# A banded attention in pieces of 128, 96 and 8 keys, four heads at a time, in front of two mixture-of-experts layers

## The chip, the cores and the metric

The kernel runs on one core of a Trainium2 chip. The time is that of one execution on the device, in microseconds; smaller is better. The core's engines are named as the profile names them: PE (TensorE, matrix products; PEld is its weight load), DVE (VectorE), ACT (ScalarE), POOL (GpSimd) and SP, which here only issues DMAs. Each engine takes its instructions in the order of the program and stops at one that has to wait.

## The reference

Attention over 2 batches, 8 heads, 768 positions and 64 numbers per head; its output, 1536 rows of 512, goes through a first mixture of 8 experts, whose weights come out of eight rounds of normalising (Sinkhorn), and a second one, in which each row goes to one expert.

```python
def _attn_ref(q, k, v, n_global, n_local):          # n_global 8, n_local 96
    scores = scale * np.matmul(q, k.transpose(0, 1, 3, 2))
    rel = pos[:, None] - pos[None, :]
    is_global = pos[None, :] < int(n_global)
    is_local = (rel >= 0) & (rel < int(n_local))
    keep = is_global | is_local
    dist = np.where(is_global & ~is_local, float(n_local), np.abs(rel))
    scores = np.where(keep, scores - slopes * dist, -1e9)
    a = softmax(scores)
    return np.matmul(a, v)
def _moe_ref(x, w_gate, w1, w2):
    P = sinkhorn(x @ w_gate)                          # 8 rounds over rows and columns
    for e in range(E):
        out += P[:, e:e + 1] * (np.maximum(x @ w1[e], 0.0) @ w2[e])
```

A query thus sees the 8 first keys and the 96 last ones up to its own. The second layer is the same two products on the rows that a greedy choice gives to each expert.

## The kernel before

The work has five stages: attention, Sinkhorn, the first layer (`hidden` and `expert_out`, by expert and by 512 rows), routing, and the second layer. Everything in the layers is done with float32 split into two half-precision parts, three products for one (`mm3`, L474 to L479).

Attention goes by 12 blocks of 128 queries (2 batches times 6). A block's keys are the 8 global ones, then 95 of the block before it, then its own 128: 231 columns (128 for the first block of a batch, whose table differs). They are kept in two pieces of 128 and 103. `load` (L213) fetches q, k and v of a block on SP's queue; v goes to `vb` in runs that end where a piece ends, so three DMAs of 8, 120 and 103 rows (L223). `qb` and `kb` have 2 buffers, `vb` has 3. `start` (L228) transposes q and k on PE; q is copied into two tiles of 128 rows whose other half is zero (`qtz`, L240), so that one head of a pair can be multiplied with all 128 rows of the pair's keys. `assemble` (L256) copies the keys into a `slab` on POOL.

A step handles two heads. `weigh` (L270): two score products on PE (L281), for each head an add of the bias table with a minimum (L284, DVE) and the exponential with its sum (L286, ACT), then the reciprocal (L288, L289, DVE) and the multiplication by it (L291, POOL). Two steps later `turn` (L293) transposes the weights on PE (L302) and copies them out of PSUM (L305 on DVE, L307 on ACT); two steps after that `mix` (L310) multiplies them with v (L319). Score banks in PSUM are two, by turns. When a block is whole, `split_x` (L322) takes a bound of its magnitudes on ACT (L499), turns it over PE (L103) into a power of two on DVE, and writes the two half-precision parts of x transposed (L333, L334) and the first gate's logits.

Between the steps stand parts of other stages: the first expert's two weight matrices (`early`, L416 loads, L420 the largest magnitude, L431 and L432 the two parts), in blocks 1 to 5 and 6 to 10, and from block 6 on two of the 16 pieces of the first expert's `hidden` per block, 14 in all. A program (the tile framework's scheduler) then sets the order on each engine; no order is written by hand.

After attention come the rest of `hidden` for expert 0, Sinkhorn (L519 to L539), and `expert_out(0, 0)`, whose DVE instruction (L572) needs Sinkhorn's result.

Of the kernel before, what the change touches and what calls it, by code (L numbers as in the profile page):

```python
# [10 lines left out]
F32 = mybir.dt.float32  # L11
# [29 lines left out]
def tile_sparse_attention_moe_moe(ctx, tc, q, k, v, ng, nl, wg1, w11, w12, wg2, w21, w22, out, taps=None):  # L41
# [19 lines left out]
    wide = WMAX > 240 or ng > P  # L61
# [53 lines left out]
    def split_gate(pool, g, kc, name):  # L115
        """[P, kc, (lo, hi, 0), E] fp16 parts of g and the scale."""
# [15 lines left out]
    def gate_product(hi, lo, hl, n, f, dst, plus=None):  # L132
        """dst[128, E] = f * sum over n chunks of (hi + lo)^T (g_hi + g_lo) [+ plus]."""
# [11 lines left out]
    def gate_block(hi, lo, sx, gw, dst):  # L145
        """dst[128 tokens, E] = x @ w_gate; hi, lo: kc -> [128, 128 tokens]."""
# [5 lines left out]
    # ------------------------------------------------------------- attention  # L152
# [6 lines left out]
    def attention(atp, aps):  # L159
        qtz = []  # L160
# [7 lines left out]
        def table(i):  # L168
            """-(bias) of the kept scores, 1e9 elsewhere, for the columns of block i."""
# [43 lines left out]
        def load(b, i):  # L213
            qb = rows(q, b, i, "qb")
            kb = rows(k, b, i, "kb") if not wide else None
            nch = (widths[i] + P - 1) // P
            vb = atp.tile([P, NCHM, H, D], F32, name="vb", bufs=3 if not wide else 2)
# [8 lines left out]
            return qb, kb, vb, nch  # L226

        def start(b, i):  # L228
            """Transposes of the block's queries and keys, and the keys that it sees."""
            c = b * NBLK + i  # L230
            qb, kb, vb, nch = lds.pop((b, i))
# [9 lines left out]
            if kb is not None:  # L241
                turn_keys(b, i, kb)
            return S

        def turn_keys(b, i, kb):
# [4 lines left out]
            if b == 0 and i < 4:  # L250
                nc.scalar.activation(kt, pt, AF.Copy)
            else:
                nc.vector.tensor_copy(kt, pt)
# [16 lines left out]
        def weigh(S, p):  # L270
            """The softmax of two heads' scores."""
            W = S.W
            ex = S.ex[p] = atp.tile([P, 2, WMAX], F32, name="ex", bufs=5 if not wide else 2)
# [20 lines left out]
        def turn(S, p):  # L294
            ex = S.ex.pop(p)
            ets = S.et[p] = []
            for a0 in range(0, S.nch, 2):
                pe = aps.tile([P, 2, 2, P], F32, name="pe", tag="tr", bufs=trb)
                for a in range(a0, min(S.nch, a0 + 2)):
# [3 lines left out]
                    et = atp.tile([P, 2, P], F32, name="et", bufs=4 if not wide else NCHM + 2)  # L303
# [6 lines left out]
        def mix(S, p):  # L310
            if p == 0:
                if S.c % 2 and not wide:
                    S.pa = mmbank([P, HP, P], name="pa")
                else:
                    S.pa = aps.tile([P, HP, P], F32, name="pa", tag="av", bufs=1)
# [6 lines left out]
        def split_x(c, pa):  # L322
            """The block's x^T in two parts and its logits, by steps."""
# [15 lines left out]

        order = [(b, i) for b in range(B) for i in range(NBLK)]  # L340
        lds = {}
        if wide:
            for b in range(B):
                for i in range(NBLK):
                    turn_keys(b, i, rows(k, b, i, "kb"))
                for i in range(NBLK):
                    lds[b, i] = load(b, i)
                    S = start(b, i)
                    assemble(S)
                    for p in range(HP):  # L350
                        weigh(S, p)
                        turn(S, p)
                        mix(S, p)
                    finish(split_x(S.c, S.pa))
            return
        warm = sml.tile([P, 1], F32, name="warm", bufs=1)
        nc.scalar.activation(warm, ones[:, 0:1], AF.Exp)
        lds[order[0]] = load(*order[0])
        table(0)
        table(min(1, NBLK - 1))  # L360
        blocks = {0: start(*order[0])}
        assemble(blocks[0])
        pairs = [(n, p) for n in range(len(order)) for p in range(HP)]
        splits = []
        with nullcontext():
            for t in range(len(pairs) + 4):
                n, p = divmod(t, HP)
                if n < len(order) and p == 0:
                    for m in (n + 1, n + 2):
                        if m < len(order) and m not in blocks and order[m] not in lds:  # L370
                            lds[order[m]] = load(*order[m])
                for z, (c0, c1, ps_) in enumerate(((1, 6, range(HP)), (6, 11, range(HP)))):
                    if c0 <= n < c1 and p in ps_:
                        next(early[z], None)
                    if (n, p) == (c1, 0):
                        finish(early[z])
                for x in splits:
                    next(x, None)
                if t < len(pairs):
                    weigh(blocks[n], p)  # L380
                if p == 0 and n + 1 < len(order):
                    blocks[n + 1] = start(*order[n + 1])
                    assemble(blocks[n + 1])
                if 0 <= t - 2 < len(pairs):
                    m, pp = pairs[t - 2]
                    turn(blocks[m], pp)
# [583 lines left out]
```

## Time and profile before

| | us |
|---|---|
| median of 3 runs | 1442.07 (1438.77 to 1445.28) |
| span of the profiled execution | 1442.0 (1442.01 with two digits) |
| first matrix product | 10.37 |
| last product of attention with v ends | 220.07 |
| first layer, routing and second layer | the rest |

The page gives no other time of the profiled execution than its span, which is 0.06 us from the median of the timed runs, so a sum made against the span is a sum against the median. Busy time is a union over an engine's instructions. In the windows, PEclk is the mean granted clock of PE, 1.00 being full, and DMA share is the mean busy share of the core's 16 DMA engines. In a wait row stand the total, the number of waits and the longest. A timeline row starts with its start and its duration, and ends with the idle time before it and what ended it. A float32 product that is no transpose has two records in the trace.

### The profile page before, as it was taken

The page shows a single profiled execution, that of the slowest core. Times are in us where ns is not written, and L with a number is a line of the kernel's source. Part 1 is how long each engine was busy: PE and PEld are TensorE (multiplying, and loading weights), DVE is VectorE, ACT ScalarE, POOL GpSimd, SP SyncE. Part 2 cuts the span into 40 slices and gives each one's busy share as a digit, 9 for nine tenths or more (in the row PEclk, how much of TensorE's full clock was granted, in tenths as well). Part 3 has the DMA queues.
Part 4 walks back from the last instruction along what each step waited for, and adds up shares of the span by engine and source line. Part 5 has one row for each costly group of instructions (what it writes and reads, how often), then busy time and mean ns, then how long its engine had stood idle before and what let it go on. Part 6 is the DMA issues. An engine that isn't in the chain of part 4 may idle for free.

```text
span 1442.0 us, 20217 instructions
## 1 busy us (share of the span) xinstructions
PE 1362.6 (94%) x7966; PEld 700.3 (49%) x7966; DVE 811.8 (56%) x1900; ACT 605.7 (42%) x1111; POOL 155.4 (11%) x289
## 2 busy tenths in 40 slices
PE   5777989999999999999999999999999999979998
PEld 4554654444444444444444444445555343337775
DVE  5555758656466656646665664575645786822111
ACT  4454745124324333432433353256553464613332
POOL 3232411101000100100010010000000000030000
PEclk9789989999999999999999999999999999999999
DMA  4444311334244415424441543341001111258640
GB/s 78 114 81 115 81 33 59 126 109 133 101 152 155 161 59 175 134 100 152 155 161 59 168 140 102 132 153 67 2 1 60 59 59 59 117 153 322 263 197 30
DMA packets 88332, 164.93 MB, mean 114 GB/s; under 512 B 49838, under 2 KB 49838, under 8 KB 85678
## 3 DMA queue, kind: packets, MB, share of 16 engines
q1 hardware_dynamic: 76814, 119.60, 26.5%
q0 software_dynamic: 11424, 44.05, 8.2%
q8 instruction: 62, 1.02, 0.3%
q14 instruction: 32, 0.26, 0.1%
HBM read 119.59 MB, written 44.05 MB: 113 GB/s over the span
## 4 chain that ended last, share of the span: by engine, by line
PE 55%; issue 13%; DMA 12%; DVE 10%; ACT 4%; SPq 3%; POOL 2%; POOLq 0%; ACTq 0%; DVEq 0%
PE py L477 9%; PE py L478 9%; PE py L479 9%; DMA raw<-in_moe_w_dram 8%; PE ph L477 6%; PE ph L479 6%; PE ph L478 6%; DMA ws<-spill 4%; DVE wam L420 2%; PE pr L761 2%; DVE wslot L432 2%; PE ps L281 2%; PE pa L319 1%; SPq L210 1%; DVE hslot L472 1%
## 5 line engine op out<-in xcount | busy, mean ns | idle before, releaser
L477 PE MATMUL py<-wslot,hslot 128*128 128x512 f16 x768 | 291.3, 379 | 9.5 <-ACT relu L471 9.0
L477 PE MATMUL ph<-xt,wslot 128*128 128x512 f16 x768 | 292.1, 380 | 0.8 <-DVE acc L574 0.7
L478 PE MATMUL ph<-xt,wslot 128*128 128x512 f16 x768 | 291.8, 380 | 0.0
L479 PE MATMUL ph<-xt,wslot 128*128 128x512 f16 x768 | 291.8, 380 | 0.0
L478 PE MATMUL py<-wslot,hslot 128*128 128x512 f16 x768 | 291.2, 379 | 0.0
L479 PE MATMUL py<-wslot,hslot 128*128 128x512 f16 x768 | 291.2, 379 | 0.0
L420 DVE TENSOR_REDUCE wam<-raw 128x1 f32<-128x1024 f32 (+1 forms) x136 | 153.1, 1151 | 93.1 <-DMA raw<-in_moe_w_dram 92.5
L470 ACT ACTIVATE hslot<-ph 128x512 f16<-128x512 f32 x192 | 114.4, 596 | 205.1 <-PE ph L479 204.9
L472 DVE TENSOR_TENSOR hslot<-relu,hslot 128x512 f16<-128x512 f32 x192 | 131.5, 688 | 112.8 <-ACT relu L471 111.9
L431 ACT ACTIVATE spill<-raw,s 128x1024 f16<-128x1024 f32 x64 | 72.9, 1147 | 235.8 <-DVE s L112 126.2
L432 DVE SCALAR_TENSOR_TENSOR spill<-raw,s,spill 128x1024 f16<-128x1024 f32 x64 | 81.6, 1283 | 108.5 <-ACT spill L431 107.3
L471 ACT ACTIVATE relu<-ph 128x512 f32<-128x512 f32 (+1 forms) x224 | 130.0, 580 | 0.0
L478 PEld LDWEIGHTS <-hslot 128*128 128x128 f16 x768 | 75.0, 98 | 100.8 <-issue 19.4
L477 PEld LDWEIGHTS <-hslot 128*128 128x128 f16 x768 | 75.0, 98 | 92.0 <-issue 10.3
L479 PEld LDWEIGHTS <-hslot 128*128 128x128 f16 x768 | 75.0, 98 | 89.9 <-issue 6.5
L479 PEld LDWEIGHTS <-wslot 128*128 128x128 f16 x768 | 75.2, 98 | 86.8 <-issue 0.8
L477 PEld LDWEIGHTS <-wslot 128*128 128x128 f16 x768 | 75.2, 98 | 86.6 <-issue 3.2
L478 PEld LDWEIGHTS <-wslot 128*128 128x128 f16 x768 | 75.2, 98 | 86.4 <-issue 2.6
L431 ACT ACTIVATE wslot<-raw,s 128x1024 f16<-128x1024 f32 (+1 forms) x72 | 71.5, 1047 | 73.1 <-PE py L479 72.6
L432 DVE SCALAR_TENSOR_TENSOR wslot<-raw,s,wslot 128x1024 f16<-128x1024 f32 (+1 forms) x72 | 81.7, 1163 | 5.0 <-ACT wslot L431 5.0
L574 DVE SCALAR_TENSOR_TENSOR acc<-py,pf,acc 128x512 f32<-128x512 f32 x84 | 61.4, 745 | 32.4 <-PE py L479 32.4
L463 POOL DMA_DIRECT2D ws<-spill x64 | 44.3, 694 | 214.8 <-DVE spill L432 214.5
(235 smaller groups left out, 1658.9 us busy)
## 6 DMA issues: line engine op xcount, KB each, us to landing
raw<-in_moe_w_dram SPq DMA_DIRECT2D x64, 1024.0 KB
ws<-spill POOLq DMA_DIRECT2D x64, 512.0 KB, 6.5
w2slot<-ws SPq DMA_DIRECT2D x16, 2048.0 KB
hd<-hslot POOLq DMA_DIRECT2D x2, 2048.0 KB, 7.8
hslot<-hd SPq DMA_DIRECT2D x2, 2048.0 KB
qb<-in_q_dram SPq DMA_DIRECT2D x12, 256.0 KB
kb<-in_k_dram SPq DMA_DIRECT2D x12, 256.0 KB
vb<-in_v_dram SPq DMA_DIRECT2D x12, 240.0 KB
```

The costliest lines, as they stand in the source:

```text
L281: nc.tensor.matmul(ps[:, j - j0, n0:n1], S.qz[:, j, p, :], S.slab[:, p, n0:n1], start=True, stop=True)
L420: nc.vector.tensor_reduce(am[:, y:y + 1], raw, axis=AX.X, op=ALU.max, apply_absolute_value=True)
L431: nc.scalar.activation(hi, raw, AF.Copy, scale=s[:, 0:1])
L432: nc.vector.scalar_tensor_tensor(lo, raw, s[:, 0:1], hi, op0=ALU.mult, op1=ALU.subtract)
L463: nc.gpsimd.dma_start(dr[:, :, a * q4:a * q4 + q4], t)
L470: nc.scalar.activation(hi, ps, AF.Relu, scale=HS)
L471: nc.scalar.activation(r[:, :n], ps, AF.Relu, scale=HS)
L472: nc.vector.tensor_sub(lo, r[:, :n], hi)
L477: nc.tensor.matmul(out_, lhs(0, a), rhs(0, a), start=a == 0, stop=False)
L478: nc.tensor.matmul(out_, lhs(0, a), rhs(1, a), start=False, stop=False)
L479: nc.tensor.matmul(out_, lhs(1, a), rhs(0, a), start=False, stop=a == n - 1)
L574: nc.vector.scalar_tensor_tensor(acc[:, c, :DM], ps, pf[:, c:c + 1], acc[:, c, :DM], op0=ALU.mult, op1=ALU.add)
```

## The change

The attention is rewritten for the case that a band and a few global keys are kept; the old function stays for other shapes and is not called. What is new:

- A block's keys stand in the order own 128, previous 96, global 8 (232 columns). v's own 128 rows (`vo`, 8 buffers) are loaded once per block, seven blocks ahead; the 96 and the 8 rows go to `vp` (3 buffers). `qb` and `kb` have 3 buffers. Keys reach the `slab` directly from PSUM by one DVE copy; POOL copies 96 and 8 columns from the slab before.
- q is not padded: one copy `qt`, and the two heads of a pair are multiplied in the upper and the lower 64 rows of the array (`tile_position`), each into its own PSUM bank.
- A step handles four heads: `turn` comes one step later, `mix` two. Each of the two score banks (`sc0`, `sc1`) has one buffer. Copies out of PSUM are 512 wide, not 256.
- The order in `mix` alternates the two halves of the output.
- The scale of x is one power of two per batch, from the largest magnitude of v (`magnitude`, a DVE reduction per block; `batch_scale`), instead of one per block from x itself.
- One more piece of `hidden`, 15, is placed between the steps. The table for 232 columns is made on POOL, clipped at 1e9.

```diff
-            vb = atp.tile([P, NCHM, H, D], F32, name="vb", bufs=3 if not wide else 2)
-                    nc.sync.dma_start(vb[p0:p0 + n, ch], v[b, :, s:s + n, :].rearrange("h p d -> p h d"))
+        def load_own(n):
+            if n < NB:
+                vos[n] = rows(v, n, "vo", 8)
+        def load(n):
+            qbs[n] = rows(q, n, "qb", 3)
+            kbs[n] = rows(k, n, "kb", 3)
+            b, i = order[n]
+            if i:
+                t = atp.tile([P, H, D], F32, name="vp", bufs=3)
+                nc.sync.dma_start(t[0:NP], v[b, :, i * P - NP:i * P, :].rearrange("h p d -> p h d"))
+                nc.sync.dma_start(t[NP:NP + ng], v[b, :, 0:ng, :].rearrange("h p d -> p h d"))
...
+            nc.vector.tensor_reduce(vams[b][:, i:i + 1], vos[n], axis=AX.XY, op=ALU.max, apply_absolute_value=True)
+        def batch_scale(b):
+            am = vams.pop(b)
+            nc.vector.tensor_reduce(am[:, NBLK:], am[:, :NBLK], axis=AX.X, op=ALU.max)
+            s = pow2_scale(am[:, NBLK:], "sv", bufs=2)
...
+            S.qt = atp.tile([P, HP, P], F32, name="qt", bufs=2)
+            nc.scalar.activation(S.qt, pt, AF.Copy, scale=qs)
+            nc.vector.tensor_copy(S.slab[:, :, 0:P], pt)
+                nc.gpsimd.tensor_copy(S.slab[:, :, P:P + NP], slabs.pop(n - 1)[:, :, P - NP:P])
+                nc.gpsimd.tensor_copy(S.slab[:, :, P + NP:], kgs[b])
...
-                ps = aps.tile([P, SJ, SW], F32, name="ps", tag="sc", bufs=2 if SW <= 256 else 1)
-                        nc.tensor.matmul(ps[:, j - j0, n0:n1], S.qz[:, j, p, :], S.slab[:, p, n0:n1],
+            ps = [aps.tile([P, 2, 256], F32, name=f"ps{j}", tag=f"sc{j}", bufs=1) for j in range(2)]
+            for y in range(HU):
+                for j in range(2):
+                    nc.tensor.matmul(ps[j][:, y, :W], S.qt[64 * j:64 * j + 64, HU * u + y, :],
+                                     S.slab[64 * j:64 * j + 64, HU * u + y, :W], start=True, stop=True,
+                                     tile_position=(64 * j, 0))
...
+                for a, ck in enumerate(S.cks):
+                    for j in range(2):
+                        nc.tensor.matmul(S.pa[64 * j:64 * j + 64, p, :], S.vs[a][:ck, 2 * p + j, :], ets[a][:ck, y, j, :],
+                                         start=a == 0, stop=a == S.nch - 1, tile_position=(0, 64 * j))
...
+            nc.scalar.activation(hi, S.pa, AF.Copy, scale=s[:, 0:1])
...
+        units = [(n, u) for n in range(NB) for u in range(2)]
+        for t in range(len(units) + 3):
+            if t < len(units):
+                weigh(blocks[n], u)
+            if u == 0 and n + 1 < NB:
+                blocks[n + 1] = start(n + 1)
+            if 0 <= t - 1 < len(units):
+                turn(blocks[m], x)
+            if 0 <= t - 2 < len(units):
+                mix(blocks[m], x)
+            if n >= 6 and first_hidden:
+                hidden(*first_hidden.pop(0))
```

The diff says little of the order on the engines, so two places are shown. The first is SP's queue near the start, in the kernel before: the loads of blocks 2 and 3, the first weights, and q and k of block 4.

```order
L210 DMA qb<-in_q_dram 128x8x64
L210 DMA kb<-in_k_dram 128x8x64
L223 DMA vb<-in_v_dram 8x8x64
L223 DMA vb<-in_v_dram 120x8x64
L223 DMA vb<-in_v_dram 103x8x64
L416 DMA raw<-in_moe_w_dram 128x2x1024 x2
L210 DMA qb<-in_q_dram 128x8x64
L210 DMA kb<-in_k_dram 128x8x64
```

And now, from the six further blocks of v on: the loads of blocks 2 and 3, the first weights, q and k of block 4 (L363 is `rows`, L378 and L379 the two runs of `vp`).

```order
L363 DMA vo<-in_v_dram 128x8x64 x6
L363 DMA qb<-in_q_dram 128x8x64
L363 DMA kb<-in_k_dram 128x8x64
L378 DMA vp<-in_v_dram 96x8x64
L379 DMA vp<-in_v_dram 8x8x64
L363 DMA vo<-in_v_dram 128x8x64
L603 DMA raw<-in_moe_w_dram 128x2x1024 x2
L363 DMA qb<-in_q_dram 128x8x64
```

No DMA of 103 rows is left; the weights stand behind seven more loads of v than before.

The second is PE in the middle of the first batch, before. `ps` are scores, `pe` the transposed weights, `pa` the product with v, `bc` the transpose of a bound for the scale.

```order
L281 MATMUL ps<-slab,qtz_113 128x231 x2
L302 MATMUL pe<-ident,ex 128x128 x4
L281 MATMUL ps<-slab,qtz_113 128x231
L302 MATMUL pe<-ident,ex 103x128 x2
L103 MATMUL bc<-ident,xam 128x128
L319 MATMUL pa<-et,vb 64x128
```

And now, with the buffer numbers: one unit's scores go to two banks by turns, and the weights of two earlier units follow.

```order
L465 MATMUL ps0_755<-slab_585,qt_578 128x232
L445 MATMUL pk_717<-ident_69,kb_530 128x128 x4
L465 MATMUL ps1_756<-slab_585,qt_578 128x232
L465 MATMUL ps0_755<-slab_585,qt_578 128x232
L465 MATMUL ps1_756<-slab_585,qt_578 128x232
L491 MATMUL pe_726<-ident_69,ex_612 128x128 x4
L491 MATMUL pe_733<-ident_69,ex_612 104x128 x4
L491 MATMUL pe_776<-ident_69,ex_688 128x128 x4
L491 MATMUL pe_783<-ident_69,ex_688 104x128 x4
L510 MATMUL pa_740<-et_731,vo_128 64x128 x2
```

Four score products of a unit now stand nearly together, where two stood alone; `bc` is gone from the block's rhythm, and `pe` comes in runs of 16.

More of the change, by code (lines that the diff above doesn't have):

```diff
@@ L60, in tile_sparse_attention_moe_moe @@
     none_kept = ng <= 0 and nl <= 0
-    wide = WMAX > 240 or ng > P
+    wide = not (B == 2 and S % P == 0 and NBLK > 1 and 1 <= ng and 2 <= nl and -(-(nl - 1) // 32) * 32 + ng <= P
+                and ng <= P - (nl - 1))
     SW = 256 if WMAX <= 256 else (512 if WMAX <= 512 else 1024)
@@ L214, in load @@
             qb = rows(q, b, i, "qb")
-            kb = rows(k, b, i, "kb") if not wide else None
             nch = (widths[i] + P - 1) // P
-            vb = atp.tile([P, NCHM, H, D], F32, name="vb", bufs=3 if not wide else 2)
+            vb = atp.tile([P, NCHM, H, D], F32, name="vb", bufs=2)
             c = 0
@@ L249, in turn_keys @@
             kt = atp.tile([P, HP, P], F32, name="kt", bufs=NBLK + 1)
[L250 to L253, printed above, removed]
+            nc.vector.tensor_copy(kt, pt)
             kts[b, i] = kt
@@ L272, in weigh @@
             W = S.W
-            ex = S.ex[p] = atp.tile([P, 2, WMAX], F32, name="ex", bufs=5 if not wide else 2)
+            ex = S.ex[p] = atp.tile([P, 2, WMAX], F32, name="ex", bufs=2)
             st4 = sml.tile([P, 4, 2], F32, name="st4", bufs=4)
@@ L302, in turn @@
                         nc.tensor.transpose(pe[:ck, a - a0, j, :], ex[:, j, a * P:a * P + ck], ident)
-                    et = atp.tile([P, 2, P], F32, name="et", bufs=4 if not wide else NCHM + 2)
+                    et = atp.tile([P, 2, P], F32, name="et", bufs=NCHM + 2)
                     if a % 2:
@@ L311, in mix @@
             if p == 0:
[L312 to L315, printed above, removed]
+                S.pa = aps.tile([P, HP, P], F32, name="pa", tag="av", bufs=1)
             ets = S.et.pop(p)
@@ L338, in split_x @@
                        sx, gw1, logits[:, c, :])
-        order = [(b, i) for b in range(B) for i in range(NBLK)]
[L341 to L355, printed above, removed]
+        lds = {}
@@ L356, in attention @@
         warm = sml.tile([P, 1], F32, name="warm", bufs=1)
         nc.scalar.activation(warm, ones[:, 0:1], AF.Exp)
[L358 to L363, printed above, removed]
-        splits = []
[L365 to L386, printed above, removed]
-                if 0 <= t - 4 < len(pairs):
-                    m, pp = pairs[t - 4]
-                    mix(blocks[m], pp)
-                    if pp == HP - 1:
-                        S = blocks.pop(m)
-                        splits.append(split_x(S.c, S.pa))
-                if (n, p) in [(c, p) for c in range(6, NC + 1) for p in (1, 3)]:
-                    hidden(*first_hidden.pop(0))
-            while splits:
-                finish(splits.pop(0))
@@ L512, in tile_sparse_attention_moe_moe @@
         with tc.tile_pool(name="att", bufs=1) as atp, tc.tile_pool(name="aps", bufs=1, space=PSUM) as aps:
-            attention(atp, aps)
+            band_attention(atp, aps)
     gw2 = load_gate(wg2, "wg2")
```

183 lines of the change are left out of this document (179 added, 4 removed).

## The prediction

> **What bounds the kernel now.** I read the page first: PE's share, then the slices.
>
> ```profile
> span 1442.0 us, 20217 instructions
> PE 1362.6 (94%) x7966; PEld 700.3 (49%) x7966; DVE 811.8 (56%) x1900; ACT 605.7 (42%) x1111; POOL 155.4 (11%) x289
> PE   5777989999999999999999999999999999979998
> PEclk9789989999999999999999999999999999999999
> ```
>
> PE is full except in the first six slices, at 36 us each, and there its clock is cut too. Those slices are attention, the only stage that is changed. The windows put numbers on it (columns: stretch, then busy time and count of PE, PEld, DVE, ACT, POOL, then PE's clock, the DMA share, GB/s).
>
> ```profile
> 10.40:91.00 80.60, 58.39 (x343) 43.48 (x343) 47.18 (x220) 43.94 (x136) 27.67 (x62) 0.84 0.35 86
> 91.00:220.00 129.00, 113.71 (x723) 74.94 (x724) 75.37 (x299) 70.94 (x207) 35.09 (x71) 0.90 0.31 74
> 220.00:1300.00 1080.00, 1056.23 (x5705) 483.18 (x5703) 659.30 (x1323) 442.11 (x672) 78.61 (x136) 1.00 0.33 109
> ```
>
> From 220 to 1300 PE is busy for 98% at full clock: whatever attention gains moves that block forward whole, whatever it loses moves it back. In the 209.6 us of the stage PE is idle for 209.6 - 58.4 - 113.7 = 37.5 us. What ends that idle time (the waits, PE's and DVE's, in the stage):
>
> ```profile
> PE pq L237 <- DMA qb<-in_q_dram: 16.7, 4, 5.3
> PE pe L302 <- POOL ex L291: 9.2, 5, 6.2
> PE ps L281 <- DVE st L284: 5.0, 2, 3.9
> PE bc L103 <- DVE logits L143: 3.6, 1, 3.6
> DVE wam L420 <- DMA raw<-in_moe_w_dram: 23.8, 4, 7.2
> ```
>
> 16.7 us are waits for q. The 6.2, 3.9 and 3.6 us are waits for an engine, but that engine hung on DVE, and DVE stood still for the weights; the timeline of DVE and PE shows one of the three:
>
> ```profile
> 123.56 1.87 DVE L420 TENSOR_REDUCE wam<-raw 128x1 f32<-128x512 f32 x3 [7.24 <-DMA raw<-in_moe_w_dram]
> 129.14 0.32 PE L103 MATMUL bc<-ident,xam 128*128 128x128 f32 x1 [3.62 <-DVE logits L143]
> ```
>
> So 16.7 + 13.7 = 30.4 of 37.5 us come from late DMAs. Why late, when the engines that move data are a third busy? SP's timeline and three windows:
>
> ```profile
> 24.15 12.09 SPq L210 DMA_DIRECT2D qb<-in_q_dram  x1
> 36.34 0.78 SPq L210 DMA_DIRECT2D kb<-in_k_dram  x1
> 37.21 2.24 SPq L223 DMA_DIRECT2D vb<-in_v_dram  x3
> 12.00:20.00 8.00, 6.03 (x27) 4.70 (x25) 6.82 (x36) 5.17 (x15) 2.83 (x8) 1.00 0.08 18
> 22.00:25.50 3.50, 1.61 (x10) 1.28 (x9) 2.87 (x18) 1.70 (x8) 1.84 (x6) 0.89 0.92 203
> 41.00:50.00 9.00, 9.00 (x49) 6.34 (x48) 4.21 (x23) 5.77 (x18) 3.48 (x8) 0.77 0.08 18
> ```
>
> After each set of v loads the queue moves 18 GB/s with 0.08 of 16 engines, about one engine, and SP's next issue takes 12 us. A run of 103 rows is 103 x 8 x 256 bytes = 211 KB; at 18 GB/s that is 11.7 us. In between, with the loads of q, k and the 8 and 120 rows in flight, 0.92 of the engines are busy and move 203 GB/s. I read it so: the DMA of 103 rows runs on one engine, everything that follows it waits behind it there, and ten blocks have one.
>
> **The change part by part.** *The loads.* 103 becomes 96 rows, and v's own rows are fetched far ahead. If 96 rows spread like 128, the 990 KB that a block now loads (q, k, v's own rows and the two runs) take some 5 us at those 203 GB/s, and SP is free again. PE's 30.4 us of DMA idle then shrink; I leave 4 us, because the second weight matrix is still loaded into buffers that are freed late, with DVE standing in front of it: -26. Bounds: 0, if 96 rows are as slow as 103 (96 x 8 x 256 bytes at 18 GB/s is 10.9 us), and -30. I take -26 since nothing but the row count sets the slow DMA apart. On this the Trainium skill, page "DMA: Bandwidth & Descriptors", section "Why a DMA increments its semaphore by 16 and not by 1", has a rule: a copy uses the largest number of engines up to 16 that divides its slowest dimension, and 127 rows get one. 103 is prime as well and 96 has 16; the windows above, 0.08 where one engine of 16 would be 0.06, agree; by the rule the term would be the full -30.
>
> *The clock.* It costs 0.16 x 80.6 = 12.9 us of full-speed time in the first half and 0.10 x 129 = 12.9 in the second; PE is busy for 72% and 88% of them, so 9.3 + 11.4 = 20.7 us of work. The dips lie around the idle gaps. With most gaps gone I take back 15; bounds 0 and -20.
>
> *The scores.* The timeline of PE gives their price alone and in a run:
>
> ```profile
> 69.92 0.66 PE L281 MATMUL ps<-slab,qtz 128*128 128x231 f32 x2
> 70.42 0.60 PE L302 MATMUL pe<-ident,ex 128*128 128x128 f32 x4
> 70.94 0.66 PE L319 MATMUL pa<-et,vb 103*64 103x128 f32 x8
> 71.53 0.66 PE L281 MATMUL ps<-slab,qtz 128*128 128x231 f32 x2
> 80.14 1.34 PE L281 MATMUL ps<-slab,qtz 128*128 128x231 f32 x6
> 81.32 0.60 PE L302 MATMUL pe<-ident,ex 128*103 128x128 f32 x4
> ```
>
> One product (two records) alone takes 70.42 - 69.92 = 0.50, in a run 1.18 / 3 = 0.39; 0.11 is what a change of shape costs. Four heads cost 1.8 now (between 4 x 0.39 + 0.11 and 4 x 0.50). With the two halves of the array at work together they cost 2 x 0.39 + 0.11 = 0.89, one after the other 1.67. Of the 24 units 20 are 232 wide: -18, and 4 units of 128 columns some -2. Against that, a third kind of array layout comes into the rhythm: two more changes of 0.11 in each of 24 units, +5. The sum is -15; bounds +3 (no overlap) and -20. I take the overlap since the products with v, which use two halves of the columns, show it: 8 records, four products, end 0.59 us after they began, where transposes of the same 128 columns take 0.13 each and one full product 128/231 x 0.39 = 0.22, so four in turn 0.86. The Trainium skill, page "TensorEngine Tiling (Array Packing)", promises up to twice the speed for 64 rows ("Theoretical Speedup") and says that changing the layout drains the array ("Key Properties"); the 0.11 us fit such a drain, and its length the page does not give.
>
> *Removed and added work.* Prices by line, in the stage:
>
> ```profile
> L103 PE MATMUL bc<-ident,xam 128*128 128x128 f32 x10 | 3.2, 323 | 3.6 <-DVE logits L143 3.6
> L284 DVE CUSTOM_DVE_ANT_0 ex<-ps,tab 128x231 f32<-128x231 f32 x80 | 30.4, 391 | 11.0 <-PE ps L281 9.4 <-POOL ex L291 1.6
> L286 ACT ACTIVATE ex<-ex,st 128x231 f32<-128x231 f32 x80 | 38.4, 483 | 28.7 <-DVE st L284 28.4
> L291 POOL TENSOR_SCALAR ex<-ex,st 128x231 f32<-128x231 f32 x80 | 40.5, 519 | 85.7 <-DVE st L289 48.1 <-DVE SXA L110 10.7 <-ACT ex L286 6.2
> L499 ACT ACTIVATE absj<-pa 128x512 bf16<-128x512 f32 x11 | 6.5, 591 | 4.8 <-PE pa L319 4.8
> L240 ACT ACTIVATE qtz<-pq 64x512 f32<-64x512 f32 x24 | 14.2, 590 | 25.1 <-PE pq L237 24.7
> L420 DVE TENSOR_REDUCE wam<-raw 128x1 f32<-128x512 f32 x16 | 10.2, 678 | 16.9 <-DMA raw<-in_moe_w_dram 16.9
> ```
>
> PE loses the ten transposes of the block bound: -3. ACT loses 12 x 0.59 for the bound and 12 x 0.59 of the second q copy; DVE gains 12 reductions of 512 (0.68 each, as L420) and loses the small chain of the scale, about as much. I cost these at nothing: DVE and ACT are busy for 122.6 and 114.9 us of the 209.6 and PE covers them. If that cover goes, ACT's 14 us count as gain. One more piece of `hidden` in the stage is one less behind it: 0.
>
> *The shorter pipeline.* Transposes come one unit of four heads after the scores, and each score bank has one buffer. A unit's weights pass DVE, ACT and POOL four times in a row before the last transposes can go. The nearest rows are PE's short waits for POOL:
>
> ```profile
> 100.67 0.33 PE L302 MATMUL pe<-ident,ex 128*128 128x128 f32 x1 [0.33 <-POOL ex L291]
> 101.56 0.33 PE L302 MATMUL pe<-ident,ex 128*128 128x128 f32 x1 [0.56 <-POOL ex L291]
> ```
>
> A mean of 0.45 in each of 24 units is +11. Bounds: 0, if scores, q and k of the next unit fill it, and two heads more on DVE and POOL, 2 x (0.39 + 0.52) = 1.8 x 24 = +44. I take +11 because PE's row of work per unit (some 5 us with `hidden`) is longer than that delay.
>
> *Behind the stage* Sinkhorn must stay covered.
>
> ```profile
> 218.92 1.15 PE L319 MATMUL pa<-et,vb 128*64 128x128 f32 x16
> 267.59 0.26 DVE L539 TENSOR_TENSOR PX<-Pm,SXA 128x96 f32<-128x96 f32 x1
> 220.00:270.00 50.00, 49.84 (x247) 22.67 (x246) 42.83 (x131) 22.13 (x36) 6.45 (x15) 1.00 0.26 85
> ```
>
> The chain from the last product with v (220.07) to Sinkhorn's end (267.85) takes 47.8 us and PE fills it, with 0.16 us idle. One piece of `hidden` less is 2.6 us less cover, but the last block's bound and scale (0.8 on ACT, then `bc` and its chain, some 3 us) drop out of the chain: +1.
>
> The sum is -26 - 15 - 15 - 3 + 11 + 1 = -47: **1395**. A second count starts from PE's work: 172.1 busy less 20.7 of clock is 151; less 15 and 3, plus 2.6, is 136; with 11.1 idle, 5.7 of clock and the 11, the stage takes 164 instead of 209.6, and 2.6 us less work lies behind it: -48. Counting scores without the layout changes adds 5 more. I forecast **1393**.
>
> **The rivals.** (1) *The halves take turns*: scores win nothing and the layout changes cost 3; the clock recovers half. -26 - 8 + 3 - 3 + 11 + 1 = -22: 1420. For it: no product of 64 rows is in this trace. (2) *All of it comes through*: -30 - 20 - 20 - 3 + 2 = -71: 1371. For it: PE then has some 136 us of work and little else to wait for. (3) *The loads stay slow*, so the change misses its largest effect, being as slow for 96 rows as for 103: gaps and clock stay, -15 - 3 + 11 = -7: 1435. Against it: the row-count reading above. (4) *Slower*: a unit's chain takes the place of the loads. Scores 0.89, four times 0.39, the last 0.48, the reciprocal's two 0.2 and four times 0.52 on POOL add to 5.4 us before its last transposes; the single buffers keep the next scores out until DVE is through. If only 1.7 us of PE's other work per unit (products with v, q and k) fits in, PE idles 3.7 in each of 24 units, +89 in place of +11: -47 + 78 = +31, 1473. It decides from (47 + 11) / 24 = 2.4 us of idle time per unit on; for it speaks that three engines at 55 to 82% wait for each other in order, against it that `hidden` stands in every second-half unit.
>
> **How the numbers follow.** Forecast 0.54, rivals (1) 0.17, (2) 0.17, (3) 0.06, (4) 0.06. 0.5% is 7 us, about what a measurement can tell. Forecast, (1) and (2) are faster, (3) lies at the edge: faster 0.89, same 0.05, slower 0.06. The range 1364 to 1426 leaves out (3) and (4) and what lies past (2); it takes in the scores' and the clock's bounds.
>
> **What would show it.** Right: no stretch at 18 GB/s in the stage; no 12 us issue on SP; PE's waits on q near nothing; clock above 0.95 after 20 us; two score records at the same time in the two banks, four heads in some 0.9 us; the last product with v near 170. Wrong: `pe <- POOL ex` as PE's longest wait (rival 4, or the pipeline term), scores at 1.6 us per unit (rival 1), DVE still standing for `raw` for over 10 us, or PE idle in front of `expert_out(0, 0)`.

## The result, and the profile after

The changed kernel takes 1394.86 us (median of 4 runs, 1391.35 to 1396.73) where the kernel before, on the same chip, takes 1440.84 (1438.77 to 1445.28): a ratio of 0.9675 (95% interval 0.9662 to 0.9688). Run again beside other kernels it took 1393.26 against 1442.46, a ratio of 0.9658 (0.9641 to 0.9674). The profiled run took 1396.73 us, its span is 1394.7. The changed attention saves 46 to 49 us.

The page of the changed kernel, the same lines as before:

```profile
span 1394.7 us, 19888 instructions
PE 1334.3 (96%) x7956; PEld 674.6 (48%) x7956; DVE 801.6 (57%) x1792; ACT 586.0 (42%) x1047; POOL 151.5 (11%) x282
PE   5899999999999999999999999999999999979998
PEclk8999999999999999999999999999999999989999
```

The holes of the first six slices are nearly gone; most of what is left of them lies in the first. Four windows of the changed kernel (stretch, then busy time and count of PE, PEld, DVE, ACT, POOL, then PE's clock, the DMA share, GB/s); the last product with v ends at 165.56, so the third is the rest of attention and the fourth what follows:

```profile
8.80:17.00 8.20, 5.47 (x33) 4.28 (x33) 8.04 (x47) 4.11 (x16) 4.28 (x9) 0.92 1.11 251
17.00:60.00 43.00, 34.76 (x228) 24.00 (x228) 28.70 (x105) 22.66 (x67) 21.77 (x45) 0.78 0.43 117
60.00:165.60 105.60, 101.86 (x806) 63.67 (x805) 78.71 (x268) 69.86 (x199) 35.35 (x75) 1.00 0.34 90
165.60:220.00 54.40, 54.30 (x260) 24.82 (x260) 46.39 (x134) 21.78 (x34) 6.25 (x16) 1.00 0.23 78
```

Where the queue crept at 18 GB/s right after the start, it moves 251, with 1.11 for the DMA share (the share can pass 1, since the one engine that worked at 18 GB/s already counted 0.08, more than a sixteenth). From 8.79 to 165.56 PE is idle for 2.7 + 8.2 + 3.7, about 15 us in place of 37.5. From 60 us on it is full and at full clock; 7.6 us of work still fall to the clock between 17 and 60 (0.22 x 34.76). PE's waits in the stage, and one row of DVE's groups up to 200 us:

```profile
PE pe L491 <- POOL ex L481: 5.9, 6, 3.4
PE ps L465 <- DVE st L471: 3.7, 4, 1.8
PE bc L105 <- DVE vam L423: 3.0, 1, 3.0
```

```profile
L607 DVE TENSOR_REDUCE wam<-raw 128x1 f32<-128x512 f32 x16 | 10.2, 677 | 0.0
```

No wait for q, k or v is among them, and DVE finds each piece of the first weights loaded: 0.0 us of idle time where the same sixteen reductions had stood still for 16.9. What PE waits for now is mostly the chain inside a unit (four heads: scores, table and minimum on DVE, exponential on ACT, multiplication on POOL, transposes). The unit itself, from PE's timeline of the changed kernel:

```profile
112.32 1.05 PE L465 MATMUL ps<-slab,qt 64*128 64x232 f32 x8
113.31 1.09 PE L491 MATMUL pe<-ident,ex 128*128 128x128 f32 x8
114.33 0.44 PE L510 MATMUL pa<-et,vo 128*64 128x128 f32 x4
114.60 0.39 PE L510 MATMUL pa<-et,vp 104*64 104x128 f32 x4
```

Eight records are four heads' scores; the next instruction starts 0.99 us after the first of them. The same four heads with full-array products, from a kernel that is described further down (`e3_after_padded_q`), take 1.57 to the next start:

```profile
115.28 1.73 PE L469 MATMUL ps<-slab,qtz 128*128 128x232 f32 x8
116.85 1.04 PE L494 MATMUL pe<-ident,ex 128*128 128x128 f32 x8
```

The records of the two halves start in pairs, less than 0.01 us apart (112.32 and 112.33 for the first): the halves work at the same time.

The products with v became cheaper too. From each product's start to that of PE's next one, waits included, they take 30 us of the stage in the changed kernel, and 35 in the kernel before with its loads repaired (`e1_before_96_7`, the second experiment), for the same 352 records.

Not all of the stage's gain arrives at the end. The stage ends 54.5 us earlier (165.56 for 220.07), Sinkhorn 56.4 us (211.48 for 267.85), the kernel 47. PE's waits in the first layer after Sinkhorn, changed kernel:

```profile
PE py L664 <- ACT relu L658: 9.8, 5, 2.6
PE ph L664 <- ACT relu L658: 5.7, 5, 1.7
PE ph L664 <- DVE acc L761: 1.7, 1, 1.7
```

Here `relu` stands for the copies by which ACT empties PSUM banks (the drains). Before, the first row was 9.0, the second absent, the third 0.7.

### The profile page after: what moved, and what is told of

Its sections match the earlier page's. It is cut to its first block, busy times and chain, and to the rows that moved or that the text cites. A ratio compares the mean times of both kernels' runs of the same rounds, so it can differ in the third digit from the quotient of the medians.

```text
span 1394.7 us, 19888 instructions
## 1 busy us (share of the span) xinstructions
PE 1334.3 (96%) x7956; PEld 674.6 (48%) x7956; DVE 801.6 (57%) x1792; ACT 586.0 (42%) x1047; POOL 151.5 (11%) x282
## 4 chain that ended last, share of the span: by engine, by line
PE 62%; issue 13%; DVE 9%; DMA 8%; ACT 4%; POOL 2%; POOLq 0%; ACTq 0%; DVEq 0%
PE py L664 11%; PE py L665 11%; PE py L666 11%; PE ph L664 7%; PE ph L666 7%; PE ph L665 7%; DMA raw<-in_moe_w_dram 4%; DMA ws<-spill 4%; DVE wam L607 2%; PE pr L948 2%; DVE wslot L619 2%; PE pe L491 2%; PE pa L510 2%; PE ps L465 1%; POOL ex L481 1%
## 5 line engine op out<-in xcount | busy, mean ns | idle before, releaser
L665 PEld LDWEIGHTS <-hslot 128*128 128x128 f16 x768 | 75.1, 98 | 101.2 <-issue 19.9
```

Of the source, the lines that this page charges most:

```text
L665: nc.tensor.matmul(out_, lhs(0, a), rhs(1, a), start=False, stop=False)
```

## The experiments

All edits are small, and the kernel before was timed beside each group. "The changed kernel" stands at 1393 to 1395 us in what follows.

**The same kernel again**, on one chip with the kernels of 96 and 7 rows, of 89 rows, and of padded q.

> The changed kernel once more, nothing edited, so that the runs beside it share its chip. Expected 1391 to 1398. Its trace tells whether PE's waits for the drains in the first layer (py and ph waiting for ACT relu), 9.8 + 5.7 us in the changed kernel against 9.0 + 0 before, come again: about 15 us if they belong to the program, anything from 9 to 16 if they belong to the run.

1393.26 us (1392.36 to 1395.53). The waits of `ph` for ACT came as 2.4 us instead of 5.7, those of `py` as 9.7: the waits of `py` came again, those of `ph` vary from run to run. Clock and work vary too: the clock from 17 to 60 us was 0.92 here and 0.78 in the first profile, with no gain at the end of the stage (158.5 us here, 156.8 there). PE is idle for over 8 of those 43 us in both, so its clock alone does not set the pace there.

**Only the DMA of 103 rows**, in the kernel before.

```diff
                     n = min(e - s, P - p0)
+                    n = 96 if n == 103 else n
                     nc.sync.dma_start(vb[p0:p0 + n, ch], v[b, :, s:s + n, :].rearrange("h p d -> p h d"))
```

> The kernel before with one line added: the DMA of 103 rows of v becomes two, of 96 and 7 rows. Theory (one slow DMA, on one engine, sets the loads, and the clock follows the gaps): the 18 GB/s stretches go, PE's 16.7 us of waits for q and DVE's 23.8 us for the weights fall below 5 each, half or more of the 20.7 us of clock comes back; 1441 - 26 - 12 = 1403, 1396 to 1412. Rival A (the loads are late because of their number and SP's queue, not of 103): 1436 to 1445. Rival B (idle goes, the clock does not follow): 1413 to 1418.

1406.17 us (1405.46 to 1406.65) against 1442.46: ratio 0.975 (0.9734 to 0.9767), 36 us from one line. Windows of this kernel (columns as above):

```profile
17.00:60.00 43.00, 32.72 (x206) 23.89 (x204) 30.42 (x139) 28.15 (x90) 19.13 (x42) 0.94 0.50 111
60.00:165.60 105.60, 103.55 (x721) 71.22 (x720) 79.61 (x320) 75.53 (x223) 37.91 (x76) 0.98 0.46 100
```

The clock is back with the gaps: in windows of 5 us over the whole stage it costs 4.0 us of work, where it cost 19.9 in the kernel before. PE's idle time in the stage falls from 37.5 to 13.4. Rivals A and B are both out. The time is 3 us above the theory's 1403: one long wait of PE stays (`bc` for `wam`, 6.6 us). It is not a wait for a load:

```profile
50.78 2.46 DVE L421 TENSOR_REDUCE wam<-raw 128x1 f32<-128x512 f32 x4
56.12 0.47 PE L103 MATMUL bc<-ident,wam 128*128 128x128 f32 x1 [6.57 <-DVE wam L422]
```

The weights have landed, and DVE waits for no DMA in the stage; it works through eight reductions of 0.6 us almost in a row, and PE stands behind them.

**Only slow loads**, in the changed kernel.

```diff
-                nc.sync.dma_start(t[0:NP], v[b, :, i * P - NP:i * P, :].rearrange("h p d -> p h d"))
+                r = 89
+                for a0, a1 in ((0, r), (r, NP)):
+                    if a1 > a0:
+                        nc.sync.dma_start(t[a0:a1], v[b, :, i * P - NP + a0:i * P - NP + a1, :].rearrange("h p d -> p h d"))
```

> The changed kernel with the 96 rows of the previous block loaded as 89 and 7, a prime number of rows as 103 was; all else as changed. Theory (the number of rows alone makes the DMA slow): 89 rows, 182 KB, take 10 us at 18 GB/s, on one engine that also has its share of every other load, so ten blocks cannot come faster than 13 to 15 us each; waits for q or v return and half of the loads' and the clock's terms are lost: 1395 + 20 = 1415, 1408 to 1432. Rival (loading v's own rows seven blocks ahead is what helped): 1394 to 1400.

1419.85 us (1418.31 to 1423.96), ratio 0.9853 (0.9836 to 0.9871): 27 us given back by 89 rows where 96 had been. A window, a wait of PE and SP's issues of this kernel:

```profile
8.80:17.00 8.20, 5.87 (x33) 4.58 (x33) 7.55 (x46) 3.93 (x16) 3.97 (x9) 0.98 0.08 18
```

```profile
PE pq L443 <- DMA qb<-in_q_dram: 6.4, 2, 4.9
```

```profile
5.66 11.07 SPq L381 DMA_DIRECT2D vp<-in_v_dram  x2
17.12 4.60 SPq L363 DMA_DIRECT2D vo<-in_v_dram  x6
23.67 10.77 SPq L381 DMA_DIRECT2D vp<-in_v_dram  x2
```

18 GB/s and the share of 0.08 are there again, as in the kernel before; at each block's 89 and 7 rows SP is held for 11 us, and everything behind them waits. Loading v's own rows far ahead, which was left in, does not replace the number of rows.

**Which numbers of rows are slow.** Each of the ten blocks gets another one.

```diff
+                r = {1: 96, 2: 95, 3: 94, 4: 93, 5: 92}[i] if b == 0 else {1: 91, 2: 90, 3: 89, 4: 88, 5: 80}[i]
+                for a0, a1 in ((0, r), (r, NP)):
...
```

> The changed kernel with the 96 rows of each block's previous piece cut differently in each of the ten blocks that have one: 96, 95+1, 94+2, 93+3, 92+4 in the first batch, 91+5, 90+6, 89+7, 88+8, 80+16 in the second. One look at how long the first of the two takes. Theory (the number of rows sets over how many engines a DMA is spread, by a divisor of it): 89 takes 10 us, 94 about half of that, 95 to 92 some 2 to 4 us, 96, 91, 90, 88 and 80 about 1 to 3 us as the 96 rows do now. Rival (only the size, or only a multiple of 16, counts): all but 96 and 80 alike, near 10 us. The Trainium skill, page 'DMA: Bandwidth & Descriptors', section 'Why a DMA increments its semaphore by 16 and not by 1', gives the largest divisor up to 16: 16 engines for 96 and 80, 15 for 90, 13 for 91, 11 for 88, 5 for 95, 4 for 92, 3 for 93, 2 for 94, 1 for 89. Besides, all that lies in SBUF behind the small tiles is moved up by 128 bytes by an unused tile: see the next run.

SP's timeline of this kernel: start, duration, line, the two DMAs of the block together. The order is that of the blocks, from 95 rows (first row; the next is 94) to 80 (last); the block with 96 has one DMA and stands ahead of them.

```profile
16.77 3.83 SPq L381 DMA_DIRECT2D vp<-in_v_dram  x2
22.28 6.20 SPq L381 DMA_DIRECT2D vp<-in_v_dram  x2
44.83 3.12 SPq L381 DMA_DIRECT2D vp<-in_v_dram  x2
65.36 2.38 SPq L381 DMA_DIRECT2D vp<-in_v_dram  x2
77.21 0.81 SPq L381 DMA_DIRECT2D vp<-in_v_dram  x2
87.60 0.81 SPq L381 DMA_DIRECT2D vp<-in_v_dram  x2
97.03 9.99 SPq L381 DMA_DIRECT2D vp<-in_v_dram  x2
122.95 0.81 SPq L381 DMA_DIRECT2D vp<-in_v_dram  x2
138.59 0.87 SPq L381 DMA_DIRECT2D vp<-in_v_dram  x2
```

| rows | 96 | 95 | 94 | 93 | 92 | 91 | 90 | 89 | 88 | 80 |
|---|---|---|---|---|---|---|---|---|---|---|
| SP held, us | 1.14 | 3.83 | 6.20 | 3.12 | 2.38 | 0.81 | 0.81 | 9.99 | 0.81 | 0.87 |
| DMA share in the middle of their transfer | - | 0.40 | 0.16 | 0.24 | 0.32 | 1.03 | - | 0.08 | 0.88 | - |

The size of the first DMA falls by a sixth from left to right and explains nothing; a multiple of 16 is not needed either, since 88, 90 and 91 are as fast as 80. What holds SP is not the DMA of many rows itself but the issue of the next one:

```profile
L381 SPq DMA_DIRECT2D vp<-in_v_dram x19: 249/452/9692, 6.2 to 139.0; - x19
```

Shortest, median and longest issue are in ns: the 89 rows were issued in 249, the 7 rows behind them in 9692. The hold therefore depends on what else is in the queue, and the DMA share, taken in windows of 0.4 to 7 us, is the better count: it is 0.08 for 89 rows and 5, 2, 3, 4, 13 and 11 times that for 95, 94, 93, 92, 91 and 88, the largest divisor up to 16 each time. The Trainium skill states this rule, page "DMA: Bandwidth & Descriptors", section "Why a DMA increments its semaphore by 16 and not by 1": a copy goes over the largest number of engines up to 16 that divides its slowest dimension. The trace agrees for these seven; the 96, 90 and 80 rows are over too soon, or run beside other loads, to tell 15 engines from 16. The whole kernel took 1401.4 us in its one run, 8 above the changed kernel.

**Half arrays undone.** q is padded with zeros again and each head's product uses all 128 rows. To make room the slab has 2 buffers, not 3; that was not tried alone.

```diff
-            nc.scalar.activation(S.qt, pt, AF.Copy, scale=qs)
+            for j in range(2):
+                nc.scalar.activation(S.qt[64 * j:64 * j + 64, j], pt[64 * j:64 * j + 64], AF.Copy, scale=qs)
...
-                    nc.tensor.matmul(ps[j][:, y, :W], S.qt[64 * j:64 * j + 64, HU * u + y, :],
-                                     S.slab[64 * j:64 * j + 64, HU * u + y, :W], start=True, stop=True,
-                                     tile_position=(64 * j, 0))
+                    nc.tensor.matmul(ps[j][:, y, :W], S.qt[:, j, HU * u + y, :],
+                                     S.slab[:, HU * u + y, :W], start=True, stop=True)
```

> The changed kernel with q padded with zeros again (two copies on ACT, two tiles for alternate blocks) and each head's scores as one product over all 128 rows; banks, units and order stay. To make room the slab has 2 buffers instead of 3 and the two tables share their scratch. Theory (half arrays save PE work that nothing else covers after 60 us): four heads take 1.7 us instead of 1.0, 24 units, less the clock: +16, 1407 to 1414. Rival (the units wait for DVE, ACT and POOL anyway): +0 to +5, 1394 to 1400.

1398.00 us (1395.59 to 1403.86), ratio 0.9706 (0.9684 to 0.9728): only 4.7 us by the medians and 7 by the ratios, though the scores alone keep PE busy for 12 to 13 us longer (40.0 + 4.6 us for the two forms, 28.1 + 3.2 in the changed kernel, 28.8 + 3.9 in its second run). So the theory of this run fell: where the changed kernel's PE is full, something in it must be waiting under the name of work.

**The transposes one unit later.** The lag in heads was not what the change had shortened: four heads' scores stand between a head's scores and its transposes in the kernel before (two steps of two heads) and in the changed kernel (one unit of four). What grew is the chain of one unit, four heads in a row in place of two. Here the lag is eight heads, and not, as the expectation has it, that of the kernel before.

```diff
-            if 0 <= t - 1 < len(units):
-                m, x = units[t - 1]
+            if 0 <= t - 2 < len(units):
+                m, x = units[t - 2]
                 turn(blocks[m], x)
-            if 0 <= t - 2 < len(units):
-                m, x = units[t - 2]
+            if 0 <= t - 3 < len(units):
+                m, x = units[t - 3]
                 mix(blocks[m], x)
```

> The changed kernel with the transposes of the weights one unit later (two units after the scores, products with v three after), so the lag in heads is that of the kernel before. Theory (the prediction's pipeline term): PE's waits for POOL ex (5.1 us in the second run of the changed kernel) and for DVE st (3.4) go away after the first unit: -5, 1385 to 1391. Rival (those waits come from the start, where POOL makes the table, and the longer lag costs one more unit at the end of attention): 1393 to 1400.

1383.25 us (1381.71 to 1386.29), ratio 0.9597 (0.958 to 0.9615): 10 to 12 us faster than the changed kernel, twice the 5 that were expected from PE's waits. The groups of the transposes between 60.0 and 165.6 us, first the changed kernel, then this one (count, busy time, mean of one, idle time before):

```profile
L491 PE MATMUL pe<-ident,ex 128*128 128x128 f32 x68 | 14.0, 295 | 3.7 <-POOL ex L481 2.5 <-ACT qt L442 0.2
```

```profile
L491 PE MATMUL pe<-ident,ex 128*128 128x128 f32 x68 | 10.8, 281 | 0.3 <-DVE slab L447 0.2
```

The same 68 records cover 14.0 us in one and 10.8 in the other. A record lasts 0.27 us or more, and in a run the next one starts 0.11 to 0.12 us after it (the row at 113.31), so transposes that come up to 0.27 us apart show no idle time. I read it so: the four transposes of a unit each wait a little for their own multiplication on POOL, and these waits count as busy. With 3.4 us of idle time, 6.6 us of the gain are in this row alone. The kernel with padded q has part of it:

```profile
L494 PE MATMUL pe<-ident,ex 128*128 128x128 f32 x68 | 12.8, 286 | 1.9 <-POOL ex L484 1.3
```

There 1.2 us of busy and 1.8 of idle time are gone from this row. Counted over the whole stage from each product's start to the next start, so that waits are in it, padding takes 8 us more for the scores than the two profiles of the changed kernel and gives 4 back at the transposes and 2 at the products with v. The next run tests whether that return goes away with the waits.

**Later transposes and padded q together.**

> The changed kernel with the transposes one unit later and with q padded with zeros (full-array scores). With the transposes as changed, padding q cost 4.7 us where PE's scores alone grew by 13 us. Theory (there PE waits for the units' chain anyway, so the scores' gain lies in that wait; with the transposes later it does not): 1383 + 10 = 1393, 1390 to 1397. Rival (the layout switches that half arrays need eat the rest of the gain, wherever the transposes stand): 1383 + 4 = 1387, 1384 to 1389.

1395.18 us (1392.57 to 1396.98), ratio 0.9678 (0.966 to 0.9695). Padding q now costs 12 us (1395.18 - 1383.25), where it cost 5 to 7 with the transposes one unit earlier. This is what the theory said, and not the rival, whose 1384 to 1389 lie below every run: half arrays are worth some 12 us when PE is the bound, and the changed kernel's pipeline takes 5 to 7 of them away. Each price is uncertain by about 4 us, so the difference is barely clear of the noise in the times; the traces bear it out, since here padding gives back 1 us at the transposes and none at the products with v. The price of the changes of layout can't be read from these runs: the scores differ by 11 us from start to next start, as much as the time does.

**One scale per block**, in the changed kernel.

```diff
-            s, f = scales[S.b]
+            s = SX[S.n]
+            am = sml.tile([P, 1], F32, name="xam")
+            nc.scalar.activation(xT[tb_i][:, 1, :, tcol:tcol + P], S.pa, AF.Abs, accum_out=am)
+            pow2_scale(am, None, s)
+            f = sml.tile([P, 1], F32, name="gf")
+            nc.vector.tensor_mul(f, s[:, 1:2], gw1[1][:, 1:2])
...
```

> The changed kernel with the scale of x per block again: for each block a bound of its magnitudes on ACT (0.6 us, its junk output goes where the second part of x is written next), turned over PE, and the small chain on DVE; the twelve reductions of v and the two scales per batch are gone, and with them the early wait of PE for them (bc waiting for vam, 2.6 to 3.0 us). Theory (the prediction: 3 us of PE and a chain of 3 us at the end, against DVE's twelve reductions that cost nothing): 1393 + 4 = 1397, 1395 to 1402. Rival (the batch scale costs an early stall at half clock as large as what it saves): 1389 to 1394.

1401.83 us (1397.48 to 1403.92), ratio 0.9722 (0.9697 to 0.9748), 8 us slower by the medians, 6 by the ratios, than the kernel that was timed beside it with 14 pieces. The scale per batch is worth more than its early stall costs. The stage is 15 us longer in this profile (last product with v ends at 181.0), 10 of them by the clock (18.0 us of work, 7.6 in the changed kernel), and what lies behind Sinkhorn 10 us shorter; unlike the kernel before, this one leaves no steps between the bound and its use, so PE stands at the transpose and at the gate (`pg` waiting for ACT `xt`, 4.0 us), and part of the 8 us belongs to that.

**14 pieces of `hidden` in the stage, not 15.**

```diff
-            if n >= 6 and first_hidden:
+            if n >= 6 and len(first_hidden) > 2:
```

> The changed kernel with 14 pieces of the first layer's hidden between the steps, as before, not 15. Theory (a piece is 2.6 us of PE's work wherever it stands): 1391 to 1397. Rival (the 15th piece swaps the two pairs of PSUM banks that the first layer's products take by turns, and that is why the stretch behind Sinkhorn takes 1180 to 1183 us instead of 1174): 1385 to 1389, and PE's waits for ACT relu back to 9 us.

1393.93 us (1392.54 to 1398.0), ratio 0.9682 (0.9658 to 0.9706): nothing. Behind Sinkhorn it takes 1179 us, the changed kernel 1183 and 1180 and the kernel before 1174, so the order in which the first layer's products take the PSUM banks by turns, which the 15th piece shifts, is not the reason for the longer stretch.

**The table of 232 columns on DVE.** The start of the second run of the changed kernel shows why this was tried: POOL's timeline, and one row of PE's.

```profile
15.63 2.11 POOL L408 TENSOR_SCALAR tab<-rel 128x232 f32<-128x232 f32 x2
17.84 1.42 POOL L481 TENSOR_SCALAR ex<-ex,st 128x128 f32<-128x128 f32 x4
19.34 6.31 POOL L408 TENSOR_SCALAR tab<-rel 128x232 f32<-128x232 f32 x6
25.75 3.15 POOL L481 TENSOR_SCALAR ex<-ex,st 128x128 f32<-128x128 f32 x8
```

```profile
18.26 1.53 PE L491 MATMUL pe<-ident,ex 128*128 128x128 f32 x4 [2.92 <-POOL ex L481]
```

The first units' multiplications stand behind the table, and PE's first transposes behind them.

```diff
-            eng = nc.vector if own_only else nc.gpsimd
+            eng = nc.vector
```

> The changed kernel with the bias table of 232 columns made on DVE, as the one of 128 is, not on POOL, where its eight instructions take 7.9 to 8.4 us ahead of the first units' multiplications. Theory (POOL's table is what PE waits for in the first 30 us: 2.9 us of pe waiting for POOL ex, then the scores behind it, at half clock): 1386 to 1391. Rival (DVE is as busy there, and the loads set the start): 1392 to 1398.

1390.68 us (1386.09 to 1392.17), ratio 0.9642 (0.9617 to 0.9666): 3.3 us less than the kernel with 14 pieces beside it (0.9658 to 0.9706), at the edge of what these runs separate. The longest wait of `pe` for POOL is 1.8 us, where it was 3.4 and 2.9 in the two profiles of the changed kernel.

**64 bytes lower in SBUF.** Behind Sinkhorn the changed kernel takes 1183 us, and the kernel before 1174. The order of ACT's instructions there is the same; what differs is that ACT waits up to 7.0 us, not 5.3, until a write of its scratch tile `spill` to memory is done, before it gets to the drains that PE waits for. In the runs so far those with the longer stretch had their large tiles at another address.

```diff
-                vams[b] = sml.tile([P, NBLK + 1], F32, name="vam")
+                vams[b] = sml.tile([P, NBLK + 1], F32, name="vam", bufs=1)
...
-        warm = sml.tile([P, 1], F32, name="warm", bufs=1)
+        warm = sml.tile([P, 1], F32, name="gam")
```

> The changed kernel with its large SBUF tiles 64 bytes lower, where those of the per-block-scale run lie: one small tile has 1 buffer instead of 2, another shares a buffer. No instruction is added or taken. In the seven runs whose raw, spill and relu tiles begin at 256 bytes modulo 512 the stretch from Sinkhorn's end to the end takes 1179 to 1183 us and the longest wait of ACT for the spill write is 6.5 to 7.0 us; in the three runs at 64 and 192 it takes 1173 to 1174 us and 5.3 to 5.6 us. Theory (the address does it, through slower DMAs beside one another): 1173 to 1175 behind Sinkhorn, longest spill wait under 5.7, PE's ph waits for ACT relu under 1.5, in all 1385 to 1389. Rival (the phase between attention's end and the second-layer weights does it, the address is chance): 1391 to 1396, 1179 to 1183 behind Sinkhorn.

1393.84 us (1392.76 to 1397.02), ratio 0.9675 (0.966 to 0.969), 1179.5 us behind Sinkhorn, longest wait for the write 6.5: the address is not it. The kernel with the table of rows, moved up by 128 bytes, agrees (1179.4 and 6.4).

**Three edits together**: transposes later, table on DVE, tiles lower.

> The changed kernel with the transposes one unit later, the table of 232 columns on DVE and the tiles 64 bytes lower. If the three add up: 1393 - 10 - 3 - 6 = 1374, 1371 to 1378. If the address is chance: 1378 to 1383. If the table's gain is gone once the transposes come later: 3 more.

1382.54 us (1381.46 to 1385.53), ratio 0.9601 (0.9587 to 0.9615). It is faster than both kernels, by 4.0% and, against the 1393.84 beside it, 0.8%, but not faster than the later transposes alone (1383.25; ratio 0.9597 there, 0.9601 here): neither the address nor the table adds anything that these runs can tell. Either the table's 3 us are gone once the transposes no longer stand close behind the scores, or they were smaller than they looked.

The order of the products in `mix`, the copies of 512 columns and the third buffers of q and k were not tried alone.

## Why the prediction was right

The time, 1394.86, lies 2 us above the forecast of 1393; the single terms are further off.

*The loads and the clock* (-26 and -15). Done alone they gave -36, undone alone +27, and the other 13 us come from the rest of the change together. The reading of the cause was right in each part: one DMA on one engine, SP held behind it, gaps at PE, the clock after the gaps. The size is 5 us short. Alone, the line took 24 us from PE's idle time and 13.5 from its busy time (172.2 to 158.7), which makes 37.6 in place of 41. (The loads of a block are 999 KB, not 990; nothing rests on it.) The step that fell short is the 4 us left for the late weights: the weights are not late any more, but DVE's reductions of them, which the prediction did not count as a cause of waits, hold PE for 6.6 us.

*The scores* (-15, two halves at once). The mechanism is as foreseen: 0.99 us per unit where 0.89, with one change of layout in it, and two more changes of 0.11 were counted. The term is some 12 us if PE is the bound and 5 to 7 in the kernel as changed. The step that failed is the sum: this term and the pipeline's were added as if they were independent. No run isolates the +5 for layouts. (The row of products with v that stands for the overlap ends 0.66 us after it began; 0.59 is the time to the next instruction's start. Both are below the 0.86 of four in turn.)

*The shorter pipeline* (+11). Right in size, 10 to 12 by undoing it, though the pipeline is shorter in steps only, not in heads, and wrong in where it would be seen. It was forecast as waits of `pe` for POOL; these are 5.9 us, 3.4 of them in one wait at the start, and the rest lies in waits that count as busy. The fourth rival, that the chain takes over with 3.7 us of idle time per unit, is far off: the stage has 15 us of idle time, 0.6 per unit.

*Removed work* (-3, ACT and DVE at nothing, +1 behind the stage). Together forecast at -2; the run with a scale per block puts it at -8, with the reservation made there. Of the table on POOL, 7.9 us ahead of the first units, the prediction said nothing; it costs some 3, at the edge of what the runs separate. Nor did it have a term for the products with v, which are 5 us shorter; which part of the change does that (the alternating order, or four heads at a time) is not shown.

*One more piece of* `hidden` (0): right.

*Behind the stage* (+1). PE stayed covered up to Sinkhorn, as forecast: no wait in front of `expert_out(0, 0)`. But the last 1183 us had been 1174, and 1.9 of these 9 us are the chain from the last product to Sinkhorn, which became that much shorter and covers that much less. In the stage the gain was 7 us larger than the second count's 164 (156.8), and the first layer gave that back. Two errors of opposite sign hid in a good sum, so that it came out within 2 us is in part luck.

Of the signs named in advance, these came: no 18 GB/s stretch, no issue of 12 us on SP (the longest is 5.67, for six loads), no wait for q, the scores at 0.99 us per unit, the last product with v near 170 (165.56). One of the signs of being wrong came as well: `pe` for POOL is PE's longest wait in the stage, if small in sum. This one did not come: a clock above 0.95 after 20 us; it was 0.78 between 17 and 60 us (0.92 in the second run), and 1.00 from 60 on.

What stays open is the first layer. In every profile with one scale per batch (the changed kernel and nine of its variants) the stretch behind Sinkhorn takes 1177 to 1183 us, in the three with one scale per block (the kernel before, the one with 96 and 7 rows, the variant above) 1173 to 1174. Behind Sinkhorn the order of the instructions on each engine is the same in the variant and the changed kernel, the end of attention does not decide (Sinkhorn ends at 227 us in the variant with 1173 and at 235 in the kernel with 89 rows and 1181), and the runs above speak against banks and addresses. Whether the scales themselves or the order just ahead of Sinkhorn does it was not tried.

## What to carry to other kernels

Look at the row count of each DMA before anything else when a queue stands still at a share of one engine: cut the run at a number with a large divisor up to 16, and see whether the gaps close and the clock recovers; here one such line gave 36 us, where the whole change gave 47. A term taken from PE's busy time is worth that much only where PE is the bound; a chain of short waits hides in records that count as busy, and shows when the same group's busy time is compared between two kernels. A step that handles more at a time has a longer chain of its own, and it is not enough to keep the lag in work: with four heads of lag as before, but four heads in a row in the chain, a fifth of what the change could gain was lost.

## What the runs showed of the hardware

A DMA's spread over the engines followed the divisors of its row count: a DMA share of 0.08 for 89 rows, 0.16 for 94 and 1.03 for 91, with SP held for 9.99, 6.20 and 0.81 us.

The clock's cost in the same stretch varied between profiles of one program (0.78 and 0.92 from 17 to 60 us) without moving the end of the stage. One dip is seen closely in the changed kernel; windows of 5 us:

```profile
45.00:50.00 5.00, 2.55 (x26) 1.78 (x23) 4.88 (x15) 2.28 (x8) 1.12 (x3) 0.99 0.81 184
50.00:55.00 5.00, 4.65 (x19) 3.37 (x18) 4.43 (x18) 2.45 (x8) 2.42 (x6) 0.50 0.00 2
55.00:60.00 5.00, 5.00 (x37) 3.35 (x35) 2.86 (x8) 4.10 (x9) 1.76 (x4) 0.83 0.02 4
```

PE was busy for half of the first window, with a gap of 1.77 us before its last product, and the next 5 us ran at half clock, though PE was busy for 4.65 of them. The gap stands where DVE reduces the first weights:

```profile
46.48 2.46 DVE L607 TENSOR_REDUCE wam<-raw 128x1 f32<-128x512 f32 x4
49.30 2.46 DVE L607 TENSOR_REDUCE wam<-raw 128x1 f32<-128x512 f32 x4
```

In the second run of the kernel the same reductions, a gap of 1.78 us and half clock from 52 to 57 us came again. Spreading those reductions was not tried.
